# Full-height tail matmuls with zero weights, and a 24-element pad under the early tiles

## The chip, the cores and the metric

The kernel runs on one core of one Trainium2 chip (trn2). Its time is the device time of one launch in microseconds; three runs of the kernel before gave 1618.24, 1619.23 and 1619.66 us, and the median, 1619.23 us, is what the changed kernel is compared with. Engines are named as in the profile: PE is TensorE's matmul row and PEld its weight-load row, DVE is VectorE, ACT is ScalarE, POOL is GpSimd and SP is SyncE, which here only issues DMAs. SBUF is the on-chip memory that engines read operands from, PSUM the one that matmuls write into.

## The reference

Two branches work on the same layer-normed input, and their results are multiplied. S is 2048, D 576, H 32 heads of 18, F 4608.

```python
x = A_x
xn = _layernorm(x, axis=-1)
s = _A_ref(xn, A_wqkv, A_w_phi, A_wo)          # linear attention, below
g = _silu(_B_ref(xn, B_w_gate, B_w_up, B_w_down))
return x + s * g

# _A_ref: q, k, v = xn @ wqkv; pq = q @ w_phi, pk = k @ w_phi, head by head
phi_q = concat(softmax(pq), softmax(-pq)); phi_k = concat(softmax(pk), softmax(-pk))
o = phi_q (phi_k^T v) / (phi_q sum(phi_k) + 1e-6)
return o @ wo
# _B_ref
return (silu(x @ w_gate) * (x @ w_up)) @ w_down
```

## The kernel before

**Split products.** A matmul here takes operands of the 32-bit type fp32r, which keeps fewer bits than fp32. So each operand is stored as a rounded part (hi) and the rest (lo), and a product is formed as hi·hi + hi·lo + lo·hi. The contraction over D = 576 is done in two halves of 288 = 128 + 128 + 32. For each chunk of 128 there are three matmuls; the tail of 32 is packed: the same 32 rows stand several times above each other with hi and lo parts placed so that one matmul over 96 rows gives all three products of the tail. A product over one half of D is thus seven matmuls, the last of which, the tail matmul, has 96 rows. Four helpers issue them: `xw` (line 94 of the profile; 14 matmuls over both halves of D), `v_product` (line 417), `product` (line 753), and, without tails, `three` (line 870) for the down projection.

**Stages.** (1) To about 70 us: x is normed, transposed by PE into the blocks `XB` (names X00 to X13), and the weights of k and q are folded with `w_phi`. While x is on its way, `keep_clock` (line 147) issues matmuls on a zero tile, `idle`, so that PE does not stand still. (2) To about 220 us: k and v for 16 tiles of 128 rows, with the sums `kvp` (line 329); the moving operands are `KVWH`, `KVWL`, `TH`, `TL`, the stationary ones pieces of X and of the tiles `shi` and `slo`. (3) To about 470 us: q, the division and the projection with `wo` (lines 94, 624, 630, 650). (4) From about 485 us to the end: the gate, up and down products, in units of 128 columns of F for each half of the rows. Gate and up are formed by a seven-product scheme on 2x2 blocks (`gate_up`, results in px, pw, py and pd), the down projection likewise (`strassen`, result in pd).

**Early units.** Units f = 0 to 4 are computed plainly during stages 1 to 3 (`early_weights`, `early_tile`): `raw` is loaded, split into `wh` and `wl`, used as stationary operand against X, 512 columns at a time (line 94, results pe), and h goes to `h_dram`. Their tiles lie in the pool `epool` at the right end of SBUF; the k/v stage's pool `kk` (v, phi, shi, slo, sraw) lies left of it. In the built program `raw`, `wh`, `wl`, `h`, `phi`, `v`, `shi` and `slo` begin 96 bytes past a multiple of 128, as `epool` begins at byte 203744 of a partition, where the pools of stage 1 end.

**Tail weights of the main stage.** Line 711 takes a tile `wt` of 96 partitions from a rotating pool with two buffers, for each unit; a DMA on SP fills it from `t_dram`, which stage 3 wrote through POOL's DMAs (line 590). `product` uses `w[1][:, m]`, one of its seven columns blocks, against `b[2][0:96]`.

**Order.** A scheduler with priorities places the instructions of each engine at build time; each engine then works its list strictly in order and waits at semaphores. Where a tile lies on bytes that another tile used before, its first write waits for the last readers of those bytes.

Of the kernel before, what the change touches and what calls it, by code (L numbers as in the profile page):

```python
# [9 lines left out]
F32 = mybir.dt.float32  # L10
F32R = mybir.dt.float32r
BF16 = mybir.dt.bfloat16
# [6 lines left out]
P = 128  # L19
NT = S // P  # L20
BT = 512
# [27 lines left out]
def gated_hedgehog_kernel(ctx: ExitStack, tc, x, w_qk, w_v, w_phi, wo, w_gu, w_tail, w_down, ident_in, mask_in, out):  # L49
# [5 lines left out]
    nc = tc.nc  # L55
# [3 lines left out]
    def split(hi, lo, src):  # L59
        nc.scalar.copy(hi, src)  # L60
        nc.vector.tensor_sub(lo, src, hi)  # L61
# [15 lines left out]
    t_dram = dram.tile([TAILS, 4, 3, 32, 7, P], F32, name="t_dram")  # L77
# [6 lines left out]
    def xw(ps, i, j, cols, wh, wl, stationary_x):  # L84
        pairs = []
        for k in range(2):
            b = XB[i][2 * j + k]
            for c in range(2):
                pairs += [(b[:, c, cols], w[:, k, c]) for w in (wh, wl)]
                pairs += [(b[:, 3 + c, cols], wh[:, k, c])]  # L90
            pairs += [(b[0:96, 2, cols], wh[0:96, k, 2])]
        for n, (a, b) in enumerate(pairs):
            l, r = (a, b) if stationary_x else (b, a)
            last = nc.tensor.matmul(ps, l, r, start=n == 0, stop=n == len(pairs) - 1)  # L94
        return last

    est = ctx.enter_context(ExitStack())
    epool = est.enter_context(tc.tile_pool(name="epool", bufs=2, side="right"))
    pes = ctx.enter_context(ExitStack())
    eps = pes.enter_context(tc.tile_pool(name="eps", bufs=2, space=PSUM, side="right"))  # L100
# [3 lines left out]
    def early_weights(f, *behind):  # L104
        parts = []
        for m in (0, 2):
            raw = epool.tile([P, 2, 3, P], F32, name="raw", bufs=2)
            hi = epool.tile([P, 2, 3, P], F32R, name="wh", bufs=3)
            lo = epool.tile([P, 2, 2, P], F32R, name="wl", bufs=3)
            nc.sync.dma_start(raw, w_gu[f, :, m:m + 2])  # L110
            with ExitStack() as order:
                for b in behind:
                    order.enter_context(tc.issue_after(b.ins))
                with tc.high_priority():
                    rests.append(split_rows(hi, lo, raw))
            parts.append((hi, lo))
        return parts
# [19 lines left out]
    with ExitStack() as att:  # L137
        const = att.enter_context(tc.tile_pool(name="const", bufs=1))
        ident = const.tile([P, P], F32, name="ident")
        nc.scalar.dma_start(ident, ident_in)  # L140
        idle = const.tile([P, BT], BF16, name="idle")
        nc.gpsimd.memset(idle, 0.0)
        unused = eps.tile([P, BT], F32, name="pe")

        def keep_clock(n):
            for _ in range(n):
                nc.tensor.matmul(unused, idle[:, 0:P], idle, start=True, stop=True)

        QH = const.tile([P, 2, 3, D], F32R, name="QH")
        QL = const.tile([P, 2, 2, D], F32R, name="QL")  # L150
# [4 lines left out]
        with ExitStack() as wst:  # L155
# [4 lines left out]
            with ExitStack() as pst:  # L160
# [102 lines left out]
                with tc.issue_after(last.ins):  # L263
                    keep_clock(6)
# [136 lines left out]
            def xs(k, n):  # L401
                if n < 4:
                    b, cs = XB[k // 4][n], slice(k % 4 * P, (k % 4 + 1) * P)
                    return [b[:, c, cs] for c in range(5)]
                j = n - 4
                h = his[k, j // 2 * 2]
                return [h[:, j % 2, c] for c in range(3)] + [los[k][:, j, c] for c in range(2)]
# [4 lines left out]
            def v_product(ps, x, w, first, last):  # L412
                wh, wl = vws[w]
                mm = [m for c in range(2) for m in ((x[c], wh[:, c]), (x[c], wl[:, c]), (x[3 + c], wh[:, c]))]
                mm += [(x[2][0:96], wh[0:96, 2])]
                for n, (l, r) in enumerate(mm):
                    nc.tensor.matmul(ps[:, 0:HALF], l, r, start=first and n == 0, stop=last and n == len(mm) - 1,
                                     skip_group_check=True)
# [44 lines left out]
            for p in range(8):  # L463
                k = (p + 4) % 8
# [26 lines left out]
                x = [xs(k, n) for n in range(8)]  # L491
# [34 lines left out]
        with ExitStack():  # L526
# [10 lines left out]
            for g, (o, w) in enumerate(GROUPS):  # L537
                for s in range(2):
                    d = zp[:, s, o:o + w] if g < NG - 1 else zq[:, s * w:s * w + w]
                    nc.tensor.matmul(d, zc[0:w, 2 * g + s:2 * g + s + 1].to_broadcast([w, P]), ident[0:w, 0:w],  # L540
                                     start=True, stop=True)
# [136 lines left out]
        for f, halves in [(1, (0,)), (0, (0,))] + [(f, (1, 0)) for f in range(2, EARLY)]:  # L678
            parts = first_weights.pop() if f == 1 else early_weights(
                f, *{0: read[2 * NT + 1:2 * NT + 2], 2: (read[2 * NT + 3], exps[NT + 1])}.get(f, ()))  # L680
# [3 lines left out]
    fw = ctx.enter_context(tc.tile_pool(name="fw", bufs=1))  # L684
    fp = ctx.enter_context(tc.tile_pool(name="fp", bufs=1, reuse_waits="tile"))
    acc = fp.tile([P, 4, HT // 2, HALF], F32, name="acc")

    def operands(i):

        xo = [None] * 7  # L690
        for n in (0, 6, 3, 1, 5, 4, 2):
            if n < 3:
                j = (0, 1, 3)[n]
                if i:
                    t = xpool.tile([P, 5, BT], F32R, name=f"X0{j}")
                    nc.sync.dma_start(t.bitcast(F32), a_dram[n])
                else:
                    t = XB[0][j]
                xo[n] = [t[:, c] for c in range(5)]
                continue  # L700
            j = n - 3
            t = xpool.tile([P, 5, BT], F32R, name=f"X1{j}")
            parts = 1 if i else 4
            rows = t.bitcast(F32).rearrange("p c n -> p (c n)").rearrange("p (a m) -> p a m", a=parts)
            src = sum_dram[i, :, j].rearrange("p s c n -> p (s c n)").rearrange("p (a m) -> p a m", a=parts)
            for a in range(parts):
                nc.sync.dma_start(rows[:, a], src[:, a])
            v = t.rearrange("p c n -> p (c n)").rearrange("p (s c n) -> p s c n", s=4, c=5)
            xo[n] = [v[:, :, c] for c in range(5)]
        return xo  # L710

    def gate_up_weights(i, f):

        parts, wt = {}, fw.tile([96, 7, P], F32R, name="wt", bufs=2)
        n, q = divmod(f - EARLY, 4)
        raw = i == 0 or f < FIRST[0]
        if raw:
            ld = fw.tile([P, 2, D], F32, name="ld", bufs=2).rearrange("p a b -> p (a b)")
            ld = ld[:, 0:8 * P].rearrange("p (m c n) -> p m c n", m=4, c=2)
            nc.sync.dma_start(ld, w_gu[f, :, :, 0:2])  # L720
            ts = fw.tile([P, D], F32, name="ts")[:, 0:4 * P].rearrange("p (m c n) -> p m c n", m=2, c=2)

        def ready(m, src):
            k = 1 if m == 6 else 2
            w = fw.tile([P, k, 4, P], F32R, name=f"w{k}", bufs=2 if k == 1 else 4)
            if not raw:
                nc.sync.dma_start(w.bitcast(F32), w_dram[f - EARLY, :, m:m + k])
            else:
                split(w[:, :, 0:2], w[:, :, 2:4], src)
                if i == 0 and f < NF - 1:  # L730
                    nc.sync.dma_start(w_dram[f - EARLY, :, m:m + k], w.bitcast(F32))
            for c in range(k):
                parts[m + c] = w[:, c]

        ready(0, ld[:, 0:2] if raw else None)
        nc.sync.dma_start(wt.bitcast(F32), t_dram[n, q].rearrange("b r m n -> (b r) m n"))
        if raw:
            nc.gpsimd.tensor_sub(ts[:, 0], ld[:, 2], ld[:, 0])  # L738
            nc.gpsimd.tensor_sub(ts[:, 1], ld[:, 3], ts[:, 0])
            nc.gpsimd.tensor_sub(ld[:, 2], ld[:, 3], ld[:, 2])  # L740
            nc.gpsimd.tensor_sub(ld[:, 1], ld[:, 1], ts[:, 1])  # L741
        ready(4, ts if raw else None)
        ready(2, ld[:, 2:4] if raw else None)
        held = {0: silus[-2:-1], 2: tops[0:1], 3: tops[1:2]}.get(f - FIRST[0]) if i == 0 else None
        with tc.issue_after(held[0].ins) if held else ExitStack():
            ready(6, ld[:, 1:2] if raw else None)
        return parts, wt

    def product(ps, w, m, b, first, last):
        mm = [(w[0][m][:, i], b[j]) for c in range(2) for i, j in ((c, c), (2 + c, c), (c, 3 + c))]  # L750
        mm += [(w[1][:, m], b[2][0:96])]
        for n, (l, r) in enumerate(mm):
            nc.tensor.matmul(ps, l, r, start=first and n == 0, stop=last and n == len(mm) - 1, skip_group_check=True)  # L753

# [344 lines left out]
    parts = early_weights(EARLY)  # L1099
# [5 lines left out]
    with tc.issue_after(outs[-3].ins):  # L1105
        ready = [gate_up_weights(*todo.pop(0))]
# [4 lines left out]
    for i, n, f in units:  # L1111
# [3 lines left out]
        if f >= FIRST[i]:  # L1115
            w = kept.pop() if i and kept else ready.pop(0)
# [33 lines left out]


def chunks(w):
    tails = [np.broadcast_to(w[512 + 32 * k:544 + 32 * k], (4, 32, w.shape[1])).reshape(P, -1) for k in range(2)]
    return np.stack([np.stack([w[256 * k:256 * k + P], w[256 * k + P:256 * k + 2 * P], tails[k]], 1)
                     for k in range(2)], 1)

# [25 lines left out]
```

## Time and profile before

| | |
|---|---|
| median of 3 runs | 1619.23 us |
| span of the profiled execution | 1616.8 us, 2.4 us under that median |
| granted TensorE clock | 0.999 |
| PE busy | 1606.6 us, 99% |
| PEld busy | 1428.7 us, 88% |
| DVE busy | 1171.1 us, 72% |
| ACT / POOL busy | 726.1 us, 45% / 664.2 us, 41% |
| matmuls | 9415 |

The page gives no time of the profiled execution beside its span; the span is from the first to the last instruction, and the runs' times hold some start and end around it. A matmul's duration in the profile (about 393 ns for 512 columns) is longer than the step from its start to the start of the next (about 230 ns), since matmuls are pipelined. Hence PE's busy share is nearly full by itself, and what the kernel pays for is the step. In the grouped rows the numbers behind the bar are busy time in us and the mean ns of one instruction.

### The profile page before, as it was taken

Reading aid. Unit: us, or ns where it says so; the run is one execution under the profiler, and the core shown is the slowest. Engines: PE = TensorE matmul, PEld = TensorE weight load, DVE = VectorE, ACT = ScalarE, POOL = GpSimd, SP = SyncE. Lnnn points to the kernel's source line nnn. Section 1 sums busy time; section 2 is a strip of 40 time slices with the busy share of each in tenths; the row PEclk is TensorE's granted clock in tenths of the full one; section 3 lists DMA queues with packets and bytes.
Section 4 is the critical chain, followed back from the end, with each engine's and each line's share of the span. In section 5 each row is a group of like instructions: output and inputs, shape, how many; then the busy total and the mean of one; then the engine's idle time right before and its main releaser. Section 6 shows DMA issues by size and latency. Waiting matters only on the chain.

```text
span 1616.8 us, 25312 instructions
## 1 busy us (share of the span) xinstructions
PE 1606.6 (99%) x9415; PEld 1428.7 (88%) x9415; DVE 1171.1 (72%) x1727; ACT 726.1 (45%) x1404; POOL 664.2 (41%) x714
## 2 busy tenths in 40 slices
PE   9999999999999999999999999999999999999998
PEld 6899998999988888888888888888888888888887
DVE  7777769899856778887777778635667656666577
ACT  5633344544435645444444444454343333333334
POOL 3666652334115635644545435223324324133133
PEclk9999999999999999999999999999999999999999
DMA  9522243436447554555555453965545665565445
GB/s 321 183 75 89 98 144 105 119 109 187 128 155 253 175 171 165 178 172 176 176 172 191 167 188 114 335 212 148 152 136 152 191 174 157 169 179 184 142 116 176
DMA packets 123181, 268.29 MB, mean 166 GB/s; under 512 B 12978, under 2 KB 54066, under 8 KB 121778
## 3 DMA queue, kind: packets, MB, share of 16 engines
q1 hardware_dynamic: 107612, 244.73, 46.4%
q0 software_dynamic: 3552, 12.59, 2.7%
q10 hardware_dynamic: 11894, 9.35, 1.8%
q8 instruction: 74, 1.21, 0.3%
q14 instruction: 49, 0.40, 0.1%
HBM read 167.53 MB, written 99.09 MB: 165 GB/s over the span
## 4 chain that ended last, share of the span: by engine, by line
PE 68%; DVE 1%; POOL 1%; DMA 1%; issue 0%; ACT 0%; SPq 0%; DVEq 0%; POOLq 0%
PE px L753 25%; PE pd L870 24%; PE pw L753 12%; PE py L753 6%; POOL acc L900 0%; DMA hb<-h_dram 0%; DVE hh L61 0%; PE pe L94 0%; DMA out<-acc 0%; DVE w L61 0%; POOL ha L1001 0%; PE pd L753 0%; DVE s L787 0%; POOL hb L996 0%; DVE ha L803 0%
## 5 line engine op out<-in xcount | busy, mean ns | idle before, releaser
L870 PEld LDWEIGHTS pd<-dw,hh 128*128 128x128 f32 x3012 | 427.8, 188 | 23.1 <-ACT pd L917 1.5
L870 PE MATMUL pd<-dw,hh 128*128 128x288 f32 x3012 | 443.7, 297 | 1.4 <-ACT pd L917 0.7
L753 PE MATMUL px<-X,w 128*128 128x512 f32 x1512 | 390.4, 393 | 0.0
L753 PEld LDWEIGHTS px<-X,w 128*128 128x128 f32 x1512 | 275.0, 188 | 52.7 <-ACT s L782 2.2
L753 PE MATMUL pw<-X,w 128*128 128x512 f32 x744 | 191.8, 393 | 0.0
L753 PEld LDWEIGHTS pw<-X,w 128*128 128x128 f32 x744 | 139.2, 188 | 31.0
L787 DVE TENSOR_TENSOR s<-pw,s 128x512 f32<-128x512 f32 x126 | 86.5, 688 | 100.4 <-ACT s L782 88.9
L1024 DVE TENSOR_TENSOR acc<-pd,acc 128x576 f32<-128x576 f32 x128 | 96.3, 753 | 84.4 <-PE pd L870 84.3
L782 ACT COPY s<-px 128x512 f32<-128x512 f32 x126 | 73.9, 586 | 160.5 <-PE px L753 160.4
L61 DVE TENSOR_TENSOR hh<-ha,hh 128x512 fp32r<-128x512 f32 x140 | 108.3, 800 | 22.8 <-ACT hh L60 21.3
L60 ACT CAST hh<-ha 128x512 fp32r<-128x512 f32 x140 | 82.7, 619 | 89.2 <-PE pd L870 72.4
L996 POOL TENSOR_TENSOR hb<-hb 128x512 f32<-128x512 f32 x34 | 45.9, 1351 | 164.4 <-DVE hb L799 159.1
L94 PE MATMUL pe<-X,wh 128*128 128x512 f32 (+1 forms) x340 | 108.3, 399 | 0.1
L61 DVE TENSOR_TENSOR w<-ld,w 128x512 fp32r<-128x512 f32 (+1 forms) x96 | 80.8, 844 | 37.2 <-ACT w L60 35.9
L753 PE MATMUL px<-X,wt 96*128 96x512 f32 x252 | 99.5, 395 | 0.0
L753 PE MATMUL py<-X,w 128*128 128x512 f32 x378 | 98.0, 394 | 0.0
L983 POOL TENSOR_TENSOR h<-ha,hb 128x512 f32<-128x512 f32 x34 | 44.7, 1314 | 125.7 <-DVE ha L803 95.5
L1009 POOL TENSOR_TENSOR ha<-ha 128x512 f32<-128x512 f32 x34 | 52.5, 1562 | 98.5 <-DVE hh L61 98.5
L60 ACT CAST w<-ld 128x512 fp32r<-128x512 f32 (+1 forms) x96 | 52.6, 549 | 88.1 <-POOL ld L741 56.0
L807 ACT COPY py<-px 128x512 f32<-128x512 f32 x63 | 36.0, 572 | 106.7 <-PE px L753 86.6
L738 POOL TENSOR_TENSOR ts<-ld 128x256 f32<-128x256 f32 x32 | 27.3, 854 | 130.4 <-issue 68.5
L753 PEld LDWEIGHTS py<-X,w 128*128 128x128 f32 x378 | 67.8, 188 | 11.3
(285 smaller groups left out, 3258.9 us busy)
## 6 DMA issues: line engine op xcount, KB each, us to landing
w_dram<-w SPq DMA_DIRECT2D x90, 512.0 KB
w<-w_dram SPq DMA_DIRECT2D x90, 512.0 KB
wt<-t_dram SPq DMA_DIRECT2D x62, 336.0 KB
ld<-in_B_w_gu SPq DMA_DIRECT2D x32, 512.0 KB
rt<-in_B_w_down SPq DMA_DIRECT2D x33, 288.0 KB
rb<-in_B_w_down SPq DMA_DIRECT2D x33, 288.0 KB
w_dram<-w SPq DMA_DIRECT2D x30, 256.0 KB
w<-w_dram SPq DMA_DIRECT2D x30, 256.0 KB
```

Of the source, the lines that this page charges most:

```text
L60: nc.scalar.copy(hi, src)
L61: nc.vector.tensor_sub(lo, src, hi)
L94: last = nc.tensor.matmul(ps, l, r, start=n == 0, stop=n == len(pairs) - 1)
L753: nc.tensor.matmul(ps, l, r, start=first and n == 0, stop=last and n == len(mm) - 1, skip_group_check=True)
L782: snaps.append(nc.scalar.copy(t, ps))
L787: nc.vector.tensor_add(t, ps, t)
L807: copies.append(nc.scalar.copy(yp, xp))
L870: nc.tensor.matmul(ps, l, r, start=first and n == 0 and m == 0, stop=n == len(hs) - 1 and m == 2, skip_group_check=True)
L983: sub(s, g["h"][0][0], g["h"][0][1])
L996: nc.gpsimd.tensor_add(a21, a21, g["h"][1][1])
L1009: sub(a12, a12, g["h"][0][0])
L1024: nc.vector.tensor_add(a2, pd[:, :, 0:HALF], a2)
```

## The change

Four things change. (a) Every tail matmul takes 128 rows in place of 96: the weights of rows 96 to 127 are zeros, either from the host's layout (`chunks`, which before repeated the 32 rows a fourth time) or, for the main stage, from two DVE memsets of rows 96 to 127 of two fixed tiles, wt0 and wt1, which the units use in turn. (b) A tile of 24 elements (96 bytes) is taken at the right end ahead of `epool`. In the built program `raw`, `wh`, `wl`, `h`, `phi`, `v`, `shi` and `slo` then begin at multiples of 128 bytes (`epool` at 203648). (c) Room for it: `idle` has 128 columns in place of 512, and `keep_clock` reads it four times over with a step of zero. By this the tiles behind `idle` at the left (QH, QL, KVWH, KVWL, TH, TL, the tiles of stage 3) begin 768 bytes lower; their place within 128 bytes is as before. From `acc` on, all tiles of the main stage lie where they lay. (d) wt is no longer taken from a rotating pool.

```diff
-            pairs += [(b[0:96, 2, cols], wh[0:96, k, 2])]
+            pairs += [(b[:, 2, cols], wh[:, k, 2])]
...
+    est.enter_context(tc.tile_pool(name="epad", bufs=1, side="right")).tile([P, 24], F32, name="epad")
     epool = est.enter_context(tc.tile_pool(name="epool", bufs=2, side="right"))
...
-        idle = const.tile([P, BT], BF16, name="idle")
+        idle = const.tile([P, P], BF16, name="idle")
         nc.gpsimd.memset(idle, 0.0)
...
-                nc.tensor.matmul(unused, idle[:, 0:P], idle, start=True, stop=True)
+                nc.tensor.matmul(unused, idle, idle.unsqueeze(1).to_broadcast([P, BT // P, P]), start=True, stop=True)
...
-                mm += [(x[2][0:96], wh[0:96, 2])]
+                mm += [(x[2], wh[:, 2])]
...
+    wts = [fw.tile([P, 7, P], F32R, name=f"wt{k}") for k in range(2)]
+    for wt in wts:
+        nc.vector.memset(wt[96:128].bitcast(F32), 0.0)
...
-        parts, wt = {}, fw.tile([96, 7, P], F32R, name="wt", bufs=2)
+        parts, wt = {}, wts[0]
+        wts.reverse()
...
-        nc.sync.dma_start(wt.bitcast(F32), t_dram[n, q].rearrange("b r m n -> (b r) m n"))
+        nc.sync.dma_start(wt[0:96].bitcast(F32), t_dram[n, q].rearrange("b r m n -> (b r) m n"))
...
-        mm += [(w[1][:, m], b[2][0:96])]
+        mm += [(w[1][:, m], b[2])]
...
-    tails = [np.broadcast_to(w[512 + 32 * k:544 + 32 * k], (4, 32, w.shape[1])).reshape(P, -1) for k in range(2)]
+    tails = [np.concatenate([w[512 + 32 * k:544 + 32 * k]] * 3 + [np.zeros_like(w[0:32])]) for k in range(2)]
```

Of the 9415 matmuls 699 are tails: 441 in `product`, 72 of 512 columns and 144 of 288 columns in `xw`, 42 in `v_product`. No engine's order changes but DVE's, by the two memsets. On DVE they come at the end of stage 3, where the last remainders ol of the numerators are formed ahead of the first splits of the main stage's weights. Before:

```order
L61 TENSOR_TENSOR pl<-pt,ph 72x512
L61 TENSOR_TENSOR ol<-po,oh 126x256
L132 TENSOR_TENSOR h<-pe,h 128x512
L61 TENSOR_TENSOR ol<-po,oh 126x256
L61 TENSOR_TENSOR ol<-po,oh 72x256
L61 TENSOR_TENSOR w_5326<-ld,w_5326 128x2x256
L61 TENSOR_TENSOR w_5335<-ts,w_5335 128x2x256
```

The same place on DVE now, where lines behind the new ones are five higher:

```order
L61 TENSOR_TENSOR pl<-pt,ph 72x512
L61 TENSOR_TENSOR ol<-po,oh 126x256
L133 TENSOR_TENSOR h<-pe,h 128x512
L61 TENSOR_TENSOR ol<-po,oh 126x256
L690 MEMSET wt_5222 32x896
L61 TENSOR_TENSOR ol<-po,oh 72x256
L690 MEMSET wt_5223 32x896
L61 TENSOR_TENSOR w_5333<-ld,w_5333 128x2x256
L61 TENSOR_TENSOR w_5342<-ts,w_5342 128x2x256
```

The first memset stands ahead of the last ol (72x256) and the second behind it. The first one also waits for PE: for the last matmul that writes po, on line 630.

On POOL the order stays, but some waits for the earlier users of the same bytes sit on other instructions. The first differences of down weights (td) show it; DMASW are the DMAs that POOL itself issued. Before:

```order
L133 DMA h_dram<-h 128x512 [waits DMASW5_49,DVE_49]
L984 TENSOR_TENSOR td<-acc 128x288 [waits DMAHW2_49,DMAHW1_49]
L989 TENSOR_TENSOR acc<-acc 128x288 [waits PE_49,Pool_49]
L990 TENSOR_TENSOR td<-acc 128x288 [waits Pool_49]
L991 TENSOR_TENSOR td<-td,acc 128x288 [waits DVE_49,Pool_49]
L738 TENSOR_TENSOR ts<-ld 128x256 [waits DMAHW6_49,DVE_49]
L984 TENSOR_TENSOR td<-rb,rt 128x288 [waits DMASW3_49,DMAHW0_49,DMASW2_49,DMAHW7_49,DMASW1_49,DMASW0_49]
```

And now:

```order
L134 DMA h_dram<-h 128x512 [waits DMASW5_49,DVE_49]
L989 TENSOR_TENSOR td<-acc 128x288 [waits DMASW3_49,DMAHW1_49,DMASW2_49,DMAHW2_49,DMASW1_49,DMASW0_49]
L994 TENSOR_TENSOR acc<-acc 128x288 [waits PE_49,Pool_49]
L995 TENSOR_TENSOR td<-acc 128x288 [waits Pool_49]
L996 TENSOR_TENSOR td<-td,acc 128x288 [waits DVE_49,Pool_49]
L743 TENSOR_TENSOR ts<-ld 128x256 [waits DMAHW6_49,DVE_49]
L989 TENSOR_TENSOR td<-rb,rt 128x288 [waits DMAHW7_49,DMAHW0_49]
```

The wait for POOL's own DMAs, those that stored the tails to `t_dram`, moved from the second group of td to the first, five instructions ahead.

## The prediction

> **What bounds the kernel.** I read the page's first part, then the stretches by stage, then the matmuls by form, and last the instructions in order of time at three places. The page first:
>
> ```profile
> span 1616.8 us, 25312 instructions
> PE 1606.6 (99%) x9415; PEld 1428.7 (88%) x9415; DVE 1171.1 (72%) x1727; ACT 726.1 (45%) x1404; POOL 664.2 (41%) x714
> ```
>
> Busy time by stretch (columns: length, then each engine's busy time and count, PE's granted clock, DMA share):
>
> ```profile
> 0.00:70.00 70.00, 67.32 (x397) 52.88 (x398) 51.72 (x123) 44.48 (x61) 29.82 (x58) 1.00 0.86 287
> 70.00:240.00 170.00, 169.97 (x1289) 165.78 (x1289) 123.94 (x157) 65.64 (x159) 113.88 (x114) 1.00 0.29 93
> 240.00:470.00 230.00, 229.82 (x1524) 208.73 (x1523) 200.24 (x314) 107.09 (x183) 63.39 (x128) 1.00 0.40 123
> 520.00:1560.00 1040.00, 1039.56 (x5695) 916.22 (x5694) 724.10 (x1039) 459.30 (x905) 407.36 (x368) 1.00 0.54 174
> ```
>
> PE stands still for 0.4 us of the 1040 in the main stage, 0.2 in the q stage, 0.03 in the k/v stage. No other engine is near full, and the clock is granted whole. So the time is the sum of PE's steps, start to start: a nanosecond less per step for 699 tails is 0.7 us, and work taken from any other engine is worth nothing unless PE waits for it.
>
> **The change, part by part.** *Tails, 96 to 128 rows.* Columns: busy us, mean ns of one, idle.
>
> ```profile
> L753 PE MATMUL px<-X,w 128*128 128x512 f32 x1512 | 390.4, 393 | 0.0
> L753 PE MATMUL px<-X,wt 96*128 96x512 f32 x252 | 99.5, 395 | 0.0
> L753 PE MATMUL pw<-X,w 128*128 128x512 f32 x744 | 191.8, 393 | 0.0
> L753 PE MATMUL pw<-X,wt 96*128 96x512 f32 x124 | 49.0, 395 | 0.0
> L94 PE MATMUL pe<-X,wh 128*128 128x512 f32 x272 | 98.9, 400 | 0.1
> L94 PE MATMUL p<-KVWH,X 128*128 128x288 f32 x256 | 60.7, 297 | 0.5 <-ACT xr L223 0.5
> L94 PE MATMUL pe<-X,wl 128*128 128x512 f32 x136 | 54.3, 399 | 0.0
> L650 PE MATMUL p<-WOL,oh 126*128 126x288 f32 x128 | 37.7, 295 | 0.0
> L94 PE MATMUL pe<-X,wh 96*128 96x512 f32 x68 | 26.9, 398 | 0.0
> L94 PE MATMUL p<-KVWH,X 96*128 96x288 f32 x64 | 19.0, 297 | 0.0
> L417 PE MATMUL vw<-KVWH,shi 128*128 128x288 f32 x24 | 7.1, 294 | 0.0
> L417 PE MATMUL vx<-KVWH,X 128*128 128x288 f32 x24 | 5.8, 296 | 0.0
> L417 PE MATMUL vw<-KVWH,shi 96*128 96x288 f32 x12 | 3.6, 299 | 0.0
> ```
>
> A tail lasts 395 ns against 393 in the main products (2 ns over 252 + 124 = 376 tails, 0.75 us), 2 ns less than its neighbours in the early units, the same at 288 columns in `xw`, 5 ns more in `v_product` (42 tails, 0.2 us). Starts in order of time show the step:
>
> ```profile
> 1202.36 1.56 PE L753 MATMUL py<-X,w 128*128 128x512 f32 x6
> 1203.75 0.39 PE L753 MATMUL py<-X,wt 96*128 96x512 f32 x1
> 1203.99 1.53 PE L753 MATMUL px<-X,w 128*128 128x512 f32 x6
> 1205.35 0.40 PE L753 MATMUL px<-X,wt 96*128 96x512 f32 x1
> 1205.59 0.70 PE L870 MATMUL pd<-dw,hh 128*128 128x288 f32 x4
> ```
>
> Both tails step 0.24 us. The six matmuls ahead take 1.39/6 = 232 ns and 1.36/6 = 227 ns a step. The tail is the last of its product, so its step also holds the change to another result. Per main tail the gain is thus 0 at the least (none in `xw`, and there a loss of 2 ns x 72 = 0.1 us) and 240 - 229.5 = 10 ns at the most, 441 x 10 = 4.4 us. I take the durations, which are means over hundreds: 0.75 + 0.2 - 0.1, a gain of 0.9 us.
>
> If 96 rows were another mode of the array, each tail would be drained of what ran before. A lone matmul takes 393 ns where a step is 230, so a drain costs about 160 ns, and 699 x 160 = 112 us would come free. The tail that starts at 1203.75 follows the last of the six without a hole, and so does px at 1203.99. The Trainium skill (TensorEngine Tiling (Array Packing), Key Properties) says that changing the tiling mode drains TensorE; the trace shows no such drain at a 96-row tail, so by that rule 96 rows is no other mode, and the 112 us stay out of the sum and get a chance under 0.01.
>
> *Early tiles by 96 bytes.* One unit's stretch, first and last row of four products of seven steps each (28 steps; these tails are merged with the neighbours of the same operands):
>
> ```profile
> 38.28 0.86 PE L94 MATMUL pe<-X,wh 128*128 128x512 f32 x3
> ...
> 44.83 0.86 PE L94 MATMUL pe<-X,wh 128*128 128x512 f32 x3
> ```
>
> (44.83 - 38.28)/28 = 234 ns a step, against 1.63/7 = 233 and 1.60/7 = 229 in the two main products above, whose weights lie at multiples of 128. So 504 early matmuls of 512 columns are 3 ns slower than the main ones' mean of 231: 1.5 us. By durations (400 and 399 against 393) it is 6 ns, 3.0 us, but those means hold waits of stage 1. Against a price of the address: the projection (line 650), whose operands begin 32 bytes past a multiple of 128, lasts 295 ns, and the products with shi (96 past) 294, no more than those with X at a multiple (296, 297). Bounds 0 and 3.0 us; between 0 and the step's 1.5 I take 1.0, since the 512-column steps are the matmuls concerned.
>
> An address 96 bytes past is still a multiple of 16 and of 32, and if only such lines count, the term is 0 and the span 1 us longer than my sum. The Trainium skill (SBUF — State Buffer, Specifications (TRN2)) gives SBUF lines of 16 bytes, by which the pad buys nothing; the 234 against 231 ns leave that open.
>
> *Operands moved by 768 bytes.* 1008 matmuls of `xw` at 288 columns, 294 of `v_product` and 480 of line 650, 1782 in all, read moving operands 768 bytes lower, the same place within 128. Among the rows at 288 columns (128 rows) the mean goes from 294 to 297 ns for no reason that I can name, so up to 3 ns either way, 1782 x 3 = 5.3 us if all went the same way; sums of several tiles should cancel, and I take 0.
>
> *Two memsets on DVE.* The first stands ahead of the last ol and waits for the matmul on po:
>
> ```profile
> 466.49 0.40 PE L630 MATMUL po<-pl,KVH 72*72 72x256 f32 x2
> 466.93 0.37 ACT L60 CAST oh<-po 72x256 fp32r<-72x256 f32 x1 [1.59 <-PE po L630]
> 467.33 0.42 DVE L61 TENSOR_TENSOR ol<-po,oh 72x256 fp32r<-72x256 f32 x1 [1.53 <-ACT oh L60]
> 467.85 0.32 PEld L650 LDWEIGHTS p<-WOH,ol 72*128 72x128 f32 x2
> 467.98 0.42 PE L650 MATMUL p<-WOH,ol 72*128 72x288 f32 x2
> ```
>
> ```profile
> 473.27 0.78 DVE L61 TENSOR_TENSOR w<-ld,w 128x512 fp32r<-128x512 f32 x1 [5.53 <-ACT w L60]
> L587 DVE TENSOR_TENSOR tl<-tl,th 128x896 f32<-128x896 f32 x8 | 8.7, 1084 | 0.0
> L203 DVE TENSOR_SCALAR xn<-xn,mv,rs 128x576 f32<-128x576 f32 x8 | 4.4, 585 | 0.1
> ```
>
> The trace has no such memset. DVE's row with 896 elements takes 1.08 us and reads two operands; at the lower end I put a memset as short as the 576 elements' 0.59. It starts when ACT does, 466.93, and ends between 467.5 and 468.0; ol then ends between 467.9 and 468.4 in place of 467.75, and PE loads it at 467.85. PE loses 0.1 to 0.6 us; I take 0.4. Queued behind the memset stands only this ol; the second memset lies in DVE's idle 5.53 us ahead of 473.27 and costs nothing.
>
> *The rest costs nothing.* SP's 62 loads of wt keep order and size. Moving POOL's wait for the stores of the tails ahead to the first td is free: the last of them was issued by 425.1, lands in 2.7 us, and td comes at 487.45:
>
> ```profile
> 423.55 1.54 POOL L590 DMA_DIRECT2D t_dram<-tl  x3
> t_dram<-tl POOLq DMA_DIRECT2D x32, 112.0 KB, 2.7
> 487.45 0.82 POOL L984 TENSOR_TENSOR td<-acc 128x288 f32<-128x288 f32 x1
> ```
>
> The quarter-size `idle` lets the first zero matmuls start up to 0.4 us sooner (its memset takes 0.53), yet x is the pace there: PE waits for POOL's copies of xn after them.
>
> ```profile
> 0.74 0.53 POOL L142 MEMSET idle<- 128x512 bf16 x1 [0.29 <-POOLq L1162]
> 11.11 0.64 PEld L215 LDWEIGHTS tp<-ident,xn 128*128 128x128 f32 x6 [0.22 <-POOL xn L206]
> ```
>
> *Sum:* -0.9 (tails) - 1.0 (pad) + 0.4 (memset) = -1.5 us; a span of 1615.3, and the same off the median of 1619.23: 1617.7 us.
>
> **Rivals.** *Tails and early steps all fall to the quickest.* If 96 rows and the pad are the whole of the difference, main tails gain 10 ns (4.4 us) and 504 early steps 5 ns (234 to 229, 2.5 us); with the memset -6.5 us, 1612.7. For it: 240 against 227 within one product. Against: tails of 96 rows in `xw` step no slower than their neighbours.
>
> *The shift by 768 bytes costs: slower than before.* Place: the k/v and q stages, where PE has no hole that could take it up. At the bound of 3 ns it is 1782 x 3 = 5.3 us, with the sum above +3.8, 1623.0. It decides from (3.2 + 1.5)/1782 = 2.6 ns per matmul on. For it: the rows' 294 to 297. Against: forms with different addresses would all have to move to the same side.
>
> *The change does nothing at the array.* Neither rows nor the pad matter and only the memset is left: 1619.6 us. For it: equal rows at 288 columns. This too is no change that can be told.
>
> **How the numbers follow.** About 0.2%, 3.2 us, is what can be told from no change here. The forecast (within it) gets 0.52, the third rival 0.11, likewise within; all steps to the quickest 0.27, the only one that is faster by more; the shift 0.10, slower. So faster 0.27, same 0.63, slower 0.10. The forecast's own range is 1616 to 1619. The range for 8 in 10 runs from 1612.5, which takes in the first rival's 1612.7, to 1621.0, which takes in the third rival and half of the shift; what lies outside is the upper half of the shift and a gain beyond the bounds.
>
> **What would show it.** Tails on 128 rows: durations of 393 in place of 395 ns and steps of 0.23 us. The pad: a period of seven early steps of 1.62 us in place of 1.64. The memset: a hole in PE of 0.1 to 0.6 us right after stage 3's last ol. The shift: the durations of line 650 and of `xw` at 288 columns, which should stay at 294 to 297. Wrong would be a main product that takes 1.59 us or less nearly everywhere, which only a dependence of all seven steps on the 96-row tail would give, or a new hole anywhere in the main stage.

## The result: 16 us faster

| | median, us | runs | ratio to before (95% interval) |
|---|---|---|---|
| before | 1619.45 | 4 | |
| after | 1603.26 | 4 | 0.9902 (0.989 to 0.9914) |

The kernel became 16.2 us faster, 1.0%, where 1.5 us were forecast; 1603.26 lies 9 us below the range. The span of the profiled execution is 15.1 us shorter. The page of the kernel after, first part:

```profile
span 1601.7 us, 25319 instructions
PE 1590.1 (99%) x9415; PEld 1420.7 (89%) x9415; DVE 1176.5 (73%) x1729; ACT 724.9 (45%) x1404; POOL 663.7 (41%) x714
```

The same 9415 matmuls, PE just as full, the two memsets on DVE; only the steps are shorter. The main stage in the stretches (columns as before):

```profile
520.00:1560.00 1040.00, 1039.54 (x5759) 920.82 (x5758) 736.81 (x1051) 464.33 (x916) 410.06 (x371) 1.00 0.54 175
```

PE starts 5759 matmuls in these 1040 us where it started 5695, with as little idle time (0.46 us, before 0.44) and the whole clock. So it isn't a wait that went away. The matmuls by form say which ones got shorter:

```profile
L875 PE MATMUL pd<-dw,hh 128*128 128x288 f32 x3012 | 438.5, 295 | 1.4 <-ACT pd L922 0.7 <-DVE X L1029 0.5 <-DVE hh L61 0.3
L758 PE MATMUL px<-X,w 128*128 128x512 f32 x1512 | 386.5, 390 | 0.0
L758 PE MATMUL px<-X,wt 128*128 128x512 f32 x252 | 98.1, 389 | 0.0
L94 PE MATMUL pe<-X,wh 128*128 128x512 f32 x340 | 107.0, 395 | 0.3 <-ACT wh L64 0.3
L651 PE MATMUL p<-WOL,oh 126*128 126x288 f32 x128 | 37.7, 295 | 0.0
```

The tails went from 395 to 389 ns, as hoped for. But the 128-row matmuls of the same products (`px<-X,w`), which the change does not touch, went from 393 to 390, and even the down matmuls (`pd<-dw,hh`, line 870 before, 875 now), which have no tail at all. Before, they stood so:

```profile
L870 PE MATMUL pd<-dw,hh 128*128 128x288 f32 x3012 | 443.7, 297 | 1.4 <-ACT pd L917 0.7 <-DVE X L1024 0.4 <-DVE hh L61 0.3
```

In order of time, the main stage now (two products and the runs of down matmuls around them):

```profile
1190.70 1.75 PE L875 MATMUL pd<-dw,hh 128*128 128x288 f32 x12
1192.29 1.53 PE L758 MATMUL py<-X,w 128*128 128x512 f32 x6
1193.65 0.39 PE L758 MATMUL py<-X,wt 128*128 128x512 f32 x1
1193.88 1.52 PE L758 MATMUL px<-X,w 128*128 128x512 f32 x6
1195.23 0.39 PE L758 MATMUL px<-X,wt 128*128 128x512 f32 x1
1195.46 0.83 PE L875 MATMUL pd<-dw,hh 128*128 128x288 f32 x5
```

From start to start the products take 1.59 and 1.58 us in place of 1.63 and 1.60, and the twelve down matmuls 1192.29 - 1190.70 = 1.59 us.

Matched one to one between the two traces, start to start and without the few steps that hold a wait, the 128-row steps of the products gave 6.4 us (2643 steps, 2.4 ns each), the down matmuls 5.2 us (3045 steps, 1.7 ns), the main tails themselves only 2.7 us (440 steps, 6.2 ns). That is 14.3 us, or 32 ns for each of the 441 main tails, of which four fifths lie outside the tail. The early 512-column steps gave 1.9 us, `xw` at 288 columns 0.7. Together that is 1.8 us more than the span shows; 1.2 of it went in the first 70 us, where PE starts later behind the wait for x. The trace of `main_tails` below, which leaves `idle` alone, shows the same 1.2 us there, so this is not the smaller `idle`.

### The profile page after: what moved, and what is told of

It is laid out like the page before. It is cut to its first block, busy times and chain, and to the rows that moved or that the text cites. A ratio compares the mean times of both kernels' runs of the same rounds, so it can differ in the third digit from the quotient of the medians.

```text
span 1601.7 us, 25319 instructions
## 1 busy us (share of the span) xinstructions
PE 1590.1 (99%) x9415; PEld 1420.7 (89%) x9415; DVE 1176.5 (73%) x1729; ACT 724.9 (45%) x1404; POOL 663.7 (41%) x714
## 4 chain that ended last, share of the span: by engine, by line
PE 92%; DVE 3%; POOL 2%; DMA 2%; ACT 1%; issue 1%; SPq 0%; ACTq 0%; DVEq 0%; POOLq 0%
PE pd L875 25%; PE px L758 24%; PE pw L758 12%; PE py L758 6%; PE p L94 6%; PE pe L94 5%; PE p L651 4%; PE kvp L330 2%; PE po L631 2%; PE vx L418 1%; PE pt L625 1%; POOL slo L363 1%; PE vy L94 1%; PE vx L94 1%; DMA wst<-in_A_w_qk 0%
## 5 line engine op out<-in xcount | busy, mean ns | idle before, releaser
L875 PE MATMUL pd<-dw,hh 128*128 128x288 f32 x3012 | 438.5, 295 | 1.4 <-ACT pd L922 0.7
L758 PE MATMUL px<-X,w 128*128 128x512 f32 x1512 | 386.5, 390 | 0.0
L94 PE MATMUL pe<-X,wh 128*128 128x512 f32 x340 | 107.0, 395 | 0.3 <-ACT wh L64 0.3
L758 PE MATMUL px<-X,wt 128*128 128x512 f32 x252 | 98.1, 389 | 0.0
```

Source lines behind the costliest of these rows:

```text
L875: nc.tensor.matmul(ps, l, r, start=first and n == 0 and m == 0, stop=n == len(hs) - 1 and m == 2, skip_group_check=True)
```

## Experiments

In every experiment's diff "before" and "after" are the two kernels, and what isn't shown is as in the one named. Times are medians, ratios stand against the kernel before on the same chip.

### Which part of the change

`main_tails` is the kernel before with (a) for the 441 main tails alone and (d):

```diff
+    wts = [fw.tile([P, 7, P], F32R, name=f"wt{k}") for k in range(2)]
+    for wt in wts:
+        nc.vector.memset(wt[96:128].bitcast(F32), 0.0)
...
-        parts, wt = {}, fw.tile([96, 7, P], F32R, name="wt", bufs=2)
+        parts, wt = {}, wts[0]
+        wts.reverse()
...
-        nc.sync.dma_start(wt.bitcast(F32), t_dram[n, q].rearrange("b r m n -> (b r) m n"))
+        nc.sync.dma_start(wt[0:96].bitcast(F32), t_dram[n, q].rearrange("b r m n -> (b r) m n"))
...
-        mm += [(w[1][:, m], b[2][0:96])]
+        mm += [(w[1][:, m], b[2])]
```

> The kernel before with the main stage's 441 tails alone on 128 rows (fixed wt tiles, zero rows from the memsets); early tails, pad and idle as before. Row theory (a 96-row matmul among 128-row ones slows its own step and the steps behind it, about 30 ns per main tail by the two traces): 441 x 30 ns = 13 us less, 1606 us, and the 288-column steps of the down projection quicker too. Address theory (the moved tiles did it): within 1 us of before, 1619.

`main_96` is the reverse, the kernel after with its main tails back on 96 rows:

```diff
-        mm += [(w[1][:, m], b[2])]
+        mm += [(w[1][0:96, m], b[2][0:96])]
```

> The changed kernel with the main stage's tails back on 96 rows; the fixed wt tiles, their memsets, the pad and the 128-row early tails stay. Row theory: the 13 us of the main stage come back, about 1616.5 us. Tile theory (it was the fixed tiles in place of the rotating pool, with other waits): stays at 1603 us. Address theory: stays at 1603 us.

`early_tails` is the kernel before with the other 258 tails on 128 rows, `pad_only` the kernel before with (b) and (c):

```diff
-            pairs += [(b[0:96, 2, cols], wh[0:96, k, 2])]
+            pairs += [(b[:, 2, cols], wh[:, k, 2])]
...
-                mm += [(x[2][0:96], wh[0:96, 2])]
+                mm += [(x[2], wh[:, 2])]
...
-    tails = [np.broadcast_to(w[512 + 32 * k:544 + 32 * k], (4, 32, w.shape[1])).reshape(P, -1) for k in range(2)]
+    tails = [np.concatenate([w[512 + 32 * k:544 + 32 * k]] * 3 + [np.zeros_like(w[0:32])]) for k in range(2)]
```

> The kernel before with the 258 tails of stages 1 to 3 alone on 128 rows (72 of 512 columns, 186 of 288). Row theory: by the two traces at most 2 us at 512 columns and 0.7 us at 288, less what the pad has of it: 1617 us. Address theory: 1619 us, with early steps still at 234 ns.

```diff
+    est.enter_context(tc.tile_pool(name="epad", bufs=1, side="right")).tile([P, 24], F32, name="epad")
...
-        idle = const.tile([P, BT], BF16, name="idle")
+        idle = const.tile([P, P], BF16, name="idle")
...
-                nc.tensor.matmul(unused, idle[:, 0:P], idle, start=True, stop=True)
+                nc.tensor.matmul(unused, idle, idle.unsqueeze(1).to_broadcast([P, BT // P, P]), start=True, stop=True)
```

> The kernel before with the pad and the small idle tile alone, all tails on 96 rows. Row theory: 1619 us, early steps of 512 columns still 234 ns. Address theory: 1603 to 1606 us. If the pad has a part of the early units' gain, 1 to 2 us less than before, and early steps below 234 ns.

| | us | ratio (95%) |
|---|---|---|
| main_tails | 1606.16 | 0.9919 (0.9904 to 0.9934) |
| main_96 | 1616.91 | 0.9983 (0.9974 to 0.9993) |
| early_tails | 1618.54 | 0.9996 (0.9986 to 1.0005) |
| pad_only | 1619.04 | 0.9995 (0.9985 to 1.0004) |

The main tails alone carry 13.4 of the 16.2 us, and taking them back loses 13.7. Everything else together gives 2.7 us (`main_96`), of which neither part by itself gives anything that the times can tell. By form, `main_96` ahead of `main_tails`:

```profile
L875 PE MATMUL pd<-dw,hh 128*128 128x288 f32 x3012 | 443.4, 297 | 1.1 <-ACT pd L922 0.7 <-DVE X L1029 0.4
L758 PE MATMUL px<-X,w 128*128 128x512 f32 x1512 | 390.6, 393 | 0.0
L758 PE MATMUL px<-X,wt 96*128 96x512 f32 x252 | 99.5, 395 | 0.0
```

```profile
L874 PE MATMUL pd<-dw,hh 128*128 128x288 f32 x3012 | 438.4, 295 | 1.1 <-ACT pd L921 0.7 <-DVE X L1028 0.5
L757 PE MATMUL px<-X,w 128*128 128x512 f32 x1512 | 386.6, 390 | 0.0
L757 PE MATMUL px<-X,wt 128*128 128x512 f32 x252 | 98.1, 389 | 0.0
```

All three rows follow the height of the tail, and `main_96` differs from the kernel after in nothing but the rows that the tail matmul reads. So a tail of 96 rows among matmuls of 128 lengthens its neighbours, the down matmuls among them.

### Is it the height 96, or the change of height?

`all_96` puts all seven matmuls of the main products on 96 rows, which leaves rows 96 to 127 of the gate and up products' chunks out of the sum; `tail_126` puts the main tails on 126 rows (the two rows left out are zeros); `tail_64` on 64 rows, which leaves out one of the tail's three partial products.

```diff
+        mm = [(l[0:96], r[0:96]) for l, r in mm]
```

> The changed kernel with all seven matmuls of each main product on 96 rows, the down projection still on 128; this leaves rows 96 to 127 of the gate and up contraction out. Switch theory (the cost is a change of height between neighbours): no change inside a product, steps of 227 ns, and only the some 460 borders to the down projection cost, 1604 to 1617 us. Height theory (a matmul on 96 rows is itself slower): all 3087 steps at 233 ns or more, at least 3087 x 6 = 18 us over the changed kernel, 1621 us or more.

```diff
-        mm += [(w[1][:, m], b[2])]
+        mm += [(w[1][0:126, m], b[2][0:126])]
```

> The changed kernel with the main tails on 126 rows (two of the zero rows left out). Group theory (what matters is a group of 32 rows of the array left unused): 126 rows use all four groups, so as the changed kernel, 1603.3 us, tails stepping 227 ns. Count theory (any number of rows other than the neighbours' counts): as with 96 rows, 441 x 30 ns more, about 1616.5 us, tails at 233 ns.

```diff
-        mm += [(w[1][:, m], b[2])]
+        mm += [(w[1][0:64, m], b[2][0:64])]
```

> The changed kernel with the main tails on 64 rows; this leaves the third product of each tail (hi by lo of the last 32 columns) out. If each unused group adds to it: twice what 96 rows cost, about 1603 + 2 x 13 = 1629 us, tails near 239 ns. If it is the change alone: as with 96 rows, 1616.5 us, tails at 233 ns. Nothing below 1603.

| rows of the six, of the tail | us | ratio (95%) |
|---|---|---|
| 128, 128 (after) | 1603.26 | 0.9902 (0.989 to 0.9914) |
| 96, 96 (all_96) | 1606.12 | 0.9918 (0.9903 to 0.9933) |
| 128, 96 (main_96) | 1616.91 | 0.9983 (0.9974 to 0.9993) |
| 128, 126 (tail_126) | 1616.89 | 0.9986 (0.9977 to 0.9995) |
| 128, 64 (tail_64) | 1774.27 | 1.0955 (1.0939 to 1.0972) |

A tail that lacks two rows costs as much as one that lacks 32, and seven matmuls of 96 rows in a row run nearly as fast as seven of 128. By form, `all_96`, then `tail_126`:

```profile
L876 PE MATMUL pd<-dw,hh 128*128 128x288 f32 x3012 | 439.5, 295 | 1.1 <-ACT pd L923 0.7 <-DVE X L1030 0.5
L759 PE MATMUL px<-X,wt 96*128 96x512 f32 x252 | 98.1, 389 | 0.0
```

```profile
L875 PE MATMUL pd<-dw,hh 128*128 128x288 f32 x3012 | 443.5, 297 | 1.1 <-ACT pd L922 0.7 <-DVE X L1029 0.4
L758 PE MATMUL px<-X,wt 126*128 126x512 f32 x252 | 99.5, 395 | 0.0
```

With 96 rows throughout, a tail lasts 389 ns as at 128. So 96 rows are not slow by themselves: what costs is a matmul that differs in height from those around it. The 2.9 us by which `all_96` is behind are near what these few times can tell, but its trace puts them into the main stage, where its products border on down matmuls of 128 rows. In order of time:

```profile
1191.78 1.75 PE L876 MATMUL pd<-dw,hh 128*128 128x288 f32 x12
1193.36 1.54 PE L759 MATMUL py<-X,w 96*128 96x512 f32 x6
1194.74 0.39 PE L759 MATMUL py<-X,wt 96*128 96x512 f32 x1
1194.97 1.52 PE L759 MATMUL px<-X,w 96*128 96x512 f32 x6
```

The product behind the down run takes 1.61 us in place of 1.59. Over the main stage `all_96` loses 3.3 us, some 14 ns for each of the 230 places where products give way to down matmuls and come back. So a border between two stretches of different heights has a price too, two of them together about half that of one lone tail (some 31 ns).

64 rows are another matter. In order of time, `tail_64`:

```profile
1195.16 1.63 PE L758 MATMUL px<-X,w 128*128 128x512 f32 x6
1196.72 0.50 PE L758 MATMUL px<-X,wt 64*128 64x512 f32 x1
1197.15 1.85 PE L875 MATMUL pd<-dw,hh 128*128 128x288 f32 x12
```

The tail steps 0.43 us in place of 0.23, and the six ahead of it 1.56 us in place of 1.36. Over the run that is (1774.27 - 1603.26)/441 = 388 ns per tail. This is a drain such as the prediction priced at about 160 ns and excluded at 96 rows. Two things show it. The weights of the tail at 1196.72 are loaded only as its matmul starts, while in the kernel after those of the tail at 1193.65 are loaded at 1193.42, ahead of it. And matched with the kernel after, the step ahead of a tail is 92 ns longer, its own 201 and the one behind 106, with little beyond: some 200 ns for each of two changes, into the tail and out of it. The Trainium skill (TensorEngine Tiling (Array Packing), Key Properties) says that changing the tiling mode drains TensorE; the 388 ns at 64 rows agree with it, and the some 30 ns at 96 and 126 are no such drain.

### How far does one tail reach?

`one_96` puts back only the 63 tails of m = 0, each followed by another product:

```diff
-        mm += [(w[1][:, m], b[2])]
+        rows = 96 if m == 0 else P
+        mm += [(w[1][0:rows, m], b[2][0:rows])]
```

> The changed kernel with one tail of seven in each main unit (that of the first product, 63 in all) on 96 rows. If each costs by itself: 63 x 30 ns = 1.9 us over the changed kernel, 1605.2 us; the trace then shows over how many steps behind it the disturbance lasts. If the first switch in a unit already puts the whole unit out of step: most of the 13 us, 1612 to 1616 us.

It took 1605.01 us, 0.9911 (0.9895 to 0.9928): 1.75 us for 63 tails, 28 ns each, by times whose intervals overlap. Surer is the trace, in order of time; the first row is the tail of 96 rows:

```profile
1189.74 0.40 PE L759 MATMUL px<-X,wt 96*128 96x512 f32 x1
1189.97 1.54 PE L759 MATMUL pw<-X,w 128*128 128x512 f32 x6
1191.35 0.39 PE L759 MATMUL pw<-X,wt 128*128 128x512 f32 x1
1191.58 1.75 PE L876 MATMUL pd<-dw,hh 128*128 128x288 f32 x12
1193.16 1.53 PE L759 MATMUL py<-X,w 128*128 128x512 f32 x6
```

The product behind it takes 1.61 us, though all its matmuls have 128 rows, and the down run behind that 1.58. Over all 63, against the kernel after, the tail's own step is 5.8 ns longer, the next 9.7, then 3.5, 1.2 and nothing: 20 ns, settled within four steps of 512 columns.

From this came the question why the tails of `main_96` cost more, some 31 ns. In the kernel before, a run of twelve down matmuls takes 1607 ns in the mean, in `one_96` 1584 (230 such runs, 23 ns each, 5.3 us): behind a lone 96-row tail the steps of 288 columns do not settle. Lone is the word: in `all_96`, where the six matmuls ahead of the tail have 96 rows too, such a run takes 1590 ns. The next two runs put the tails back in two groups: `inside_96` (m = 0, 1, 6; 189 tails, of which 175 are followed by a product and 14 by down matmuls), `border_96` (m = 2 to 5; 252 tails, 216 followed by a down run).

```diff
-        mm += [(w[1][:, m], b[2])]
+        rows = 96 if m in (0, 1, 6) else P
+        mm += [(w[1][0:rows, m], b[2][0:rows])]
```

> The changed kernel with the tails of products 0, 1 and 6 on 96 rows (189 of 441), which 512-column matmuls follow. Settling theory (512-column steps settle within four steps, a run of twelve 288-column steps carries the disturbance to its end): 189 x 20 ns = 3.8 us over the changed kernel, 1607.1 us, down steps unchanged at 132.1 ns. Equal theory (each tail costs 30 ns wherever it stands): 5.7 us, 1609.0 us.

```diff
-        mm += [(w[1][:, m], b[2])]
+        rows = 96 if m in (2, 3, 4, 5) else P
+        mm += [(w[1][0:rows, m], b[2][0:rows])]
```

> The changed kernel with the tails of products 2, 3, 4 and 5 on 96 rows (252 of 441), most of which a run of down-projection matmuls follows. Settling theory: 252 tails, of which some 225 with a run of twelve 288-column steps behind them that takes 23 ns longer: 9 to 11 us over the changed kernel, 1613 us, down steps at 133.9 ns. Equal theory: 252 x 30 = 7.6 us, 1610.9 us.

`inside_96` took 1607.92 us, 0.9936 (0.9922 to 0.9951); `border_96` 1614.03, 0.9972 (0.996 to 0.9983). Against the kernel after that is 4.7 us for 189 tails, 25 ns each, and 10.8 us for 252, 43 ns each (by the ratios, which allow for the chip, 5.5 and 11.3 us, 29 and 45 ns). An equal price per tail, which would be 5.7 and 7.6 us, falls with the second; the first alone, between the 3.8 us of the one expectation and the 5.7 of the other, would not decide it. By form, `inside_96`, then `border_96`:

```profile
L876 PE MATMUL pd<-dw,hh 128*128 128x288 f32 x3012 | 438.5, 295 | 1.3 <-ACT pd L923 0.7 <-DVE X L1030 0.4 <-DVE hh L61 0.2
```

```profile
L876 PE MATMUL pd<-dw,hh 128*128 128x288 f32 x3012 | 443.3, 297 | 1.1 <-ACT pd L923 0.7 <-DVE X L1030 0.5
```

The whole loss of the down matmuls, about 5 us, is in `border_96`. Its order of time shows that it doesn't end there:

```profile
1196.13 1.52 PE L759 MATMUL pw<-X,w 128*128 128x512 f32 x6
1197.49 0.40 PE L759 MATMUL pw<-X,wt 96*128 96x512 f32 x1
1197.72 1.77 PE L876 MATMUL pd<-dw,hh 128*128 128x288 f32 x12
1199.33 1.56 PE L759 MATMUL py<-X,w 128*128 128x512 f32 x6
1200.72 0.39 PE L759 MATMUL py<-X,wt 128*128 128x512 f32 x1
1200.95 1.53 PE L759 MATMUL px<-X,w 128*128 128x512 f32 x6
```

After the 96-row tail at 1197.49 the down run takes 1.61 us, and the product `py` behind it 1.62, though it has 128 rows from its first matmul to its last; only there the disturbance settles.

### What the pad does

`no_pad` is the kernel after without the tile, so that the early tiles begin 96 bytes past a multiple of 128; `pad_32b` and `pad_64b` put them 64 and 32 bytes past.

```diff
-    est.enter_context(tc.tile_pool(name="epad", bufs=1, side="right")).tile([P, 24], F32, name="epad")
```

> The changed kernel without the pad: early tiles 96 bytes past a multiple of 128 again, all tails on 128 rows. By the early steps of 512 columns (234.8 ns with only the tails changed, 230.7 in the changed kernel) 504 x 4 = 2 us over the changed kernel, 1605.3 us, early steps back at 234 to 235 ns. If the pad is worth nothing: 1603.3 us and steps of 231.

```diff
-    est.enter_context(tc.tile_pool(name="epad", bufs=1, side="right")).tile([P, 24], F32, name="epad")
+    est.enter_context(tc.tile_pool(name="epad", bufs=1, side="right")).tile([P, 8], F32, name="epad")
```

> The changed kernel with a pad of 32 bytes: early tiles 64 bytes past a multiple of 128. If a multiple of 64 is enough: as the changed kernel, 1603.3 us, early steps at 231 ns. If it takes a multiple of 128: as without the pad, 1605.3 us and 234 to 235 ns.

```diff
-    est.enter_context(tc.tile_pool(name="epad", bufs=1, side="right")).tile([P, 24], F32, name="epad")
+    est.enter_context(tc.tile_pool(name="epad", bufs=1, side="right")).tile([P, 16], F32, name="epad")
```

> The changed kernel with a pad of 64 bytes: early tiles 32 bytes past a multiple of 128. If any address that is no multiple of 64 costs: as without the pad, 234 to 235 ns and 1605.3 us; if it is 96 bytes past alone: 231 ns and 1603.3 us.

They took 1604.86 us, 0.9916 (0.9901 to 0.993), 1605.03, 0.9915 (0.99 to 0.993), and 1604.35, 0.991 (0.9896 to 0.9925): 1.1 to 1.8 us behind the kernel after, with intervals that overlap, so the times settle nothing. The steps do. In order of time, the first and the last of some products of seven steps: after, `no_pad`, `pad_64b`, `pad_only`.

```profile
39.30 0.84 PE L94 MATMUL pe<-X,wh 128*128 128x512 f32 x3
...
44.06 0.84 PE L94 MATMUL pe<-X,wh 128*128 128x512 f32 x3
```

```profile
39.73 0.86 PE L94 MATMUL pe<-X,wh 128*128 128x512 f32 x3
...
44.65 0.86 PE L94 MATMUL pe<-X,wh 128*128 128x512 f32 x3
```

```profile
38.50 0.86 PE L94 MATMUL pe<-X,wh 128*128 128x512 f32 x3
...
45.03 0.86 PE L94 MATMUL pe<-X,wh 128*128 128x512 f32 x3
```

```profile
39.80 0.86 PE L94 MATMUL pe<-X,wh 128*128 128x512 f32 x3
...
44.64 0.86 PE L94 MATMUL pe<-X,wh 128*128 128x512 f32 x3
```

After: 4.76 us over 21 steps, 227 ns. `no_pad`: 4.92 over 21, 234 ns, as before the change. `pad_64b`: 6.53 over 28, 233 ns, and `pad_32b` the same. Matched one to one over the 504 early steps, waits left out, `no_pad` loses 1.9 us to the kernel after, `pad_32b` 1.6 and `pad_64b` 1.5, and no other form of matmul moves by more than 0.15. So 96, 64 and 32 bytes past are nearly alike, and of the four places tried only the multiple of 128 gives the short step. That every multiple of 128 would is not shown by these four. `pad_only`, whose tails have 96 rows, has 4.84 over 21, 230.5 ns, like the main products before; and `early_tails`, without the pad, stays at 234. Each of the two lengthenings hides the other in part: at 234 ns a step the tail's height costs nothing more. Matched with the kernel before, the early steps gain 0.8 us in `pad_only` and nothing in `early_tails`, against 1.9 us with both; what `early_tails` gains, 0.6 us, is at the 288 columns of `xw`, 4 ns for each of 144 tails. The Trainium skill (SBUF — State Buffer, Specifications (TRN2)) gives lines of 16 bytes, by which alone all four places would be alike; the 234 against 227 ns differ from that.

### A version that might be faster

`stage3_128` is the kernel after with the matmuls of stage 3 that have 126 or 72 rows padded to 128 with zeros (all but 48 on po), the zeros written by POOL; KVH, KVL and the operands of po are widened in the same way:

```diff
...
-            WOH = qw.tile([GW, NG, D], F32R, name="WOH")
-            WOL = qw.tile([GW, NG, D], F32R, name="WOL")
+            WOH = qw.tile([P, NG, D], F32R, name="WOH")
+            WOL = qw.tile([P, NG, D], F32R, name="WOL")
+            for t in (WOH, WOL):
+                nc.gpsimd.memset(t[96:128, 0:NG - 1].bitcast(F32), 0.0)
+                nc.gpsimd.memset(t[64:128, NG - 1].bitcast(F32), 0.0)
...
-                                nc.tensor.matmul(ps[:, 0:HALF], a[0:w, g, jc], bw[0:w, g, n], start=k == 0,
+                                nc.tensor.matmul(ps[:, 0:HALF], a[:, g, jc], bw[:, g, n], start=k == 0,
```

> The changed kernel with stage 3's matmuls of the numerators and of the projection on 128 rows too (zero rows and columns in KVH, KVL, WOH, WOL), 48 of 72 rows left. The trace of the changed kernel has 247 changes of height between neighbours, nearly all in stage 3. If each change costs as in the main stage (30 ns for a tail, two changes): some 200 x 10 to 15 ns = 2 to 3 us less than the changed kernel, 1600.5 us. If a change costs nothing at 288 columns, as the 0.7 us from 186 such tails suggest: 1603 us, or more by the memsets.

1603.03 us, 0.9902 (0.9885 to 0.9918): no change that can be told from the kernel after. The form on line 651 (657 here), at 126 rows before, lasts 295 ns either way:

```profile
L657 PE MATMUL p<-WOL,oh 128*128 128x288 f32 x160 | 47.1, 295 | 0.0
```

The traces tell more than the times here. Matched one to one, the steps of po gained 0.23 us, those of the projection 0.07 and the early steps between them 0.2: half a microsecond in all, where 2 to 3 were expected if each change cost as in the main stage. Nor did the memsets hide a larger gain, since from 70 to 490 us PE lost no time to the kernel after. So in this stage, which has changes of height throughout, they cost next to nothing; why they cost more in the main stage stays open. No version beat the kernel after.

## Why the prediction was wrong, point by point

*Right: what bounds the kernel.* The time is the sum of PE's steps. The gain came from steps, while PE's idle time in the main stage stayed below 0.5 us.

*Wrong: the tails' term.* It was -0.9 us; with the main tails on 128 rows it measured -13.4 (`main_tails`) and -13.7 (after against `main_96`). Two things in its working failed. The gain was put at the tail's own duration against its neighbours' in the same kernel (395 against 393 ns). But those neighbours were lengthened themselves, to 393 from 390 ns, so the reference was already disturbed. And the upper bound of 10 ns per tail, 4.4 us, took the tail's own step for the whole of the cost, where it is a fifth of it: 6 of 32 ns. (The 240 ns of that bound came from rows rounded to 0.01 us; the trace has 233.) The down matmuls, a third of the gain, stood in no term. The row that could have told was quoted there: two products side by side with six steps of 1.39 and of 1.36 us, the same matmuls. The quicker, 227 ns a step, was what an undisturbed one takes; the mean of the two, 229.5 ns, was used as if it were. The text named the right mechanism once, as what would make it wrong, and gave it no chance and no price: 441 products at 1.59 us, in place of seven steps of the mean 231 ns, would have been 441 x 0.027 = 12 us.

*Right for its reason, and no help: no drain at 96 rows.* The 112 us stayed out as they should; where there is a drain, at 64 rows, it is 388 ns per tail, for two changes in place of the one that was priced. But that no drain could be seen was taken as saying that a change of height costs next to nothing. Between the two lies a cost of 25 to 43 ns.

*The pad's term* was -1.0 us, from 234 against 231 ns. The steps fell to 227, since 231 too was a disturbed figure: 504 x 7 ns would be 3.5 us by the steps seen in the window, of which the matched traces show 1.9 us over all 504 and the times 1.1 to 1.8. The size is within the bounds of 0 to 3.0; that over half of it hangs on the tails of 128 rows was not foreseen. Projections that begin 32 bytes past and last 295 ns had been put against a price of the address; they have 288 columns, and the 512-column steps went another way.

*The memset's +0.4 us* did not come. Its time was within the estimate, 0.81 us, and it did stand ahead of the last ol. In order of time, DVE and then PE:

```profile
466.40 0.81 DVE L690 MEMSET wt<- 32x896 f32 x1 [1.34 <-PE po L631]
467.23 0.42 DVE L61 TENSOR_TENSOR ol<-po,oh 72x256 fp32r<-72x256 f32 x1
```

```profile
467.10 0.30 PE L651 MATMUL p<-WOL,oh 72*128 72x288 f32 x1
467.24 0.63 PE L94 MATMUL pe<-X,wh 128*128 128x512 f32 x2
467.71 0.40 PE L94 MATMUL pe<-X,wl 128*128 128x512 f32 x1
467.94 0.43 PE L651 MATMUL p<-WOH,ol 72*128 72x288 f32 x2
```

PE bridged the 0.7 us with three matmuls of the last early unit, which stood behind this ol before. The statement that no engine's order changes but DVE's was wrong: on PE some matmuls of that unit had been placed ahead, into just this gap.

*Right: the move by 768 bytes costs nothing.* Line 650's row kept its 295 ns, and `main_96`, which has the move, is not slower than before.

*The rivals.* "All fall to the quickest" was the nearest, with 1612.7 us and the right side; it priced main tails at their own 10 ns, and so ended 9 us short. The costly shift and "nothing at the array" are out.

## What to carry to other kernels

Keep neighbouring matmuls at one height: where PE is full, pad a lone odd tail with rows of zeros, since here 441 tails of 96 or 126 rows among 128 cost 13.4 us and the padded ones nothing. Expect less elsewhere: the tails of `xw` at 288 columns cost 4 ns each, and stage 3 next to nothing. When a trace seems to show that an operation costs no more than its neighbours, look whether the neighbours are at their own best: compare the quickest repeat of the same sequence (1.36 us), not the mean (1.38), and count the steps behind it too. Try stationary operands of 512-column matmuls at a multiple of 128 bytes, and measure the two changes together, since each hid the other's gain.

## What was not expected of the hardware

A single matmul of another height lengthens what follows: at 512 columns its own step by 5.8 ns, the next by 9.7, then 3.5 and 1.2; a run of twelve 288-column steps behind it by 23 ns up to its end, and the product behind that as well (1.62 in place of 1.59 us). Behind seven matmuls of 96 rows the same run loses only 6 ns. 126 rows do this as 96 do, and 64 rows cost 388 ns. Why a change of height upsets steps that follow it, no run here shows. Stationary operands off a multiple of 128 bytes, by 32, 64 or 96 alike, step 233 to 234 ns at 512 columns in place of 227.
